# A fused attention and MLP kernel: PSUM banks from one pool, and an order chosen anew every four tiles

## The chip, the core and the metric

The kernel runs on one core of one Trainium2 chip. The core has TensorE (PE, matrix products into the accumulator memory PSUM), VectorE (DVE), ScalarE (ACT), GpSimd (POOL) and SyncE (SP, which issues the transfers). The engines run side by side, each taking its own instructions in the order in which the program wrote them, and they meet through semaphores. The metric is the device time of one execution in microseconds (us).

## The reference

One input `x` of 2048 rows by 512 goes through two branches that a gate mixes row by row:

```
x = A_x
g = sigmoid((x * gate_w).sum(-1))
a = attention(x, wqkv) @ wo          # 32 heads of 16, softmax over 2048 keys
h = gelu(layernorm(x) @ w1)          # then its quarters moved by 1, -1, 2, -2 rows
x1 = x + shifted(h) @ w2
b = x1 + gelu(layernorm(x1) @ w3) @ w4     # w3 is 512 x 1792
out = g * a + (1 - g) * b
```

Most of the work is the attention: 32 heads, each with 2048 x 2048 scores of which the exponential is taken and which are then multiplied by the values.

## The kernel before

The scores are cut into 2048 tiles of 128 keys by 512 queries, in 32 rounds of 64 tiles. A round is one chunk of 512 queries (`c`), one group of eight heads (`G`) and one parity (`p`), so four heads at a time: these lie in four row strips of PE. A score tile is one matmul over 32 rows (`qk_op`, L926 to L932), and two to four of them, in different strips, run at once. The products with the values and all projections use four column strips: four matmuls at a time, each into 32 partitions of one PSUM bank. Going from one kind to the other costs PE a pause, so the program gathers both kinds in groups.

A tile's exponential is made in one of two ways. `act_tiles` and `issue_act` (L940, L997) give two tiles to ScalarE, which turns 128x1024 scores at once into probabilities (L1009, tile `PA`); each tile then needs one matmul that adds its product with the values into the round's accumulator `acc` (L1104). `dve_tile` and `issue_dve` (L974, L1019) give one tile to VectorE, whose first pass (L1035) writes a linear function of the scores as 16-bit integers that, read as bf16, approximate a power of two. Two such tiles make a pair of 128x1024 in a buffer `PD`. `close_pair` (L1048) makes three more copies of the pair with a constant added (L1071 on VectorE, L1073 on POOL), and all four go into the accumulator with weights held in `V0` and `V2`: four matmuls per tile. Who makes the copies depends on two constants. Normally VectorE makes two and POOL makes the third out of the second. For a share `GP2` of the pairs (`both`), VectorE makes one and POOL makes two, straight from the first pass. Near the end of a round, and for a share 1 - `GP3`, VectorE makes all three (`alone`). At most three pairs are in work (`token`).

PSUM has eight banks. Before, they are fixed tiles: two tiles of two banks for ScalarE units (`psA`), three single banks (`ring`) for VectorE tiles and all projections, and `acc`. At the end of a round (`finish_round`, L1112) VectorE copies `acc` out (L1120); the next round's products may start when that copy is done (`acc_ready`). Transfers then spread the row sums, and POOL divides (L1137) and SP stores the heads into `oD`.

Around the attention lie the other products, each a generator of matmul groups (`gen`, L608) with the bank it needs, a place from which it may begin (`at`) and one by which it is due: transposes of `x`, projections to `q`, `k`, `v`, the gate, the MLP products `w1`, `w2`, `w3` and `w4` with the output projection. VectorE takes their results out of PSUM (`evac`, L625). ScalarE does GELU five times in large instructions.

The order of all this is decided when the program is built. The class `Sim` keeps a model of the five engines with a duration for each job (`hold`) and a latency, and steps through time: each engine takes the ready job of the best priority whose buffers are free, and `pe_pick` (L1268) decides what PE does next. First come scores for ScalarE when a unit's banks are free, together with tiles for VectorE while a ring bank is free and fewer than `DVE_WAIT` first passes wait; then, for as long as ScalarE is busy, projections and products with the values. Instructions are written out in the order of their modelled start. POOL's jobs and VectorE's copies within SBUF are marked `port`: the model never lets two of them overlap, and each POOL instruction waits for the last such VectorE instruction written before it (`in_port_order`, L158).

Some 25 constants (`BASE`) steer these choices: priorities, how many first passes may wait, how far tiles of the next round may go ahead, how full a group of products must be. A table `STAGES` replaces some of them for each 32 tiles.

Of the kernel before, what the change touches and what calls it, by code (L numbers as in the profile page):

```python
# [47 lines left out]

class Call:
# [6 lines left out]
class Job:  # L56
    __slots__ = ("eng", "hold", "lat", "deps", "prio", "fn", "acq", "frees", "at", "done", "start", "seq", "ready", "name", "port")

    def __init__(self, eng, hold, lat, deps, fn, prio=5, acq=(), frees=(), at=0, name="", port=False):
# [6 lines left out]
        self.name = name  # L66


class Op:
    __slots__ = ("mode", "tile", "fn", "done", "start", "ns", "frees", "name")  # L70

    def __init__(self, mode, tl, fn, ns=216.0, frees=(), name=""):
        self.mode, self.tile, self.fn, self.ns, self.frees = mode, tl, fn, ns, list(frees)
        self.done = self.start = None
        self.name = name


class Gen:


    def __init__(self, units, deps, at, name, acq="ring", due=None):
# [25 lines left out]
class Sim:  # L107
# [4 lines left out]
    def __init__(self, slots):  # L112
        self.free = {k: list(v) for k, v in slots.items()}
        self.jobs = {e: [] for e in ("ACT", "DVE", "POOL", "SP")}
        self.t_free = {e: 0.0 for e in ("ACT", "DVE", "POOL", "SP", "PE")}
# [12 lines left out]
        self.pelog = []  # L128

# [4 lines left out]
    def add(self, job):  # L134
        self.n += 1
        job.seq = self.n
        self.jobs[job.eng].append(job)
        self.pending += 1
        return job

    def take(self, b):
        b.slot = self.free[b.cls].pop(0)

    def release(self, bufs):
        for b in bufs:
# [4 lines left out]
            if b.users == 0:  # L150
                self.free[b.cls].append(b.slot)

# [16 lines left out]
    def finish_job(self, job):  # L169
        job.done = self.t  # L170
        self.release(job.frees)

    def try_engine(self, e):
        if self.t_free[e] > self.t:
            return False
        best = None
        for j in self.jobs[e]:
            if j.at > self.tiles:
                continue
            if j.ready is None:  # L180
                if any(d.done is None for d in j.deps):
                    continue
                j.ready = self.t
            if any(not self.free[b.cls] for b in j.acq) or j.port and self.lock > self.t:
                continue
# [10 lines left out]
        self.emit(self.t, self.in_port_order(e, j.fn) if j.port else j.fn)  # L196
# [10 lines left out]
    def pe_run(self, ops):  # L207
        cur = self.t
        for o in ops:
# [14 lines left out]
            self.emit(s, o.fn)  # L224
# [11 lines left out]
    def finish_op(self, o):  # L236
        o.done = self.t
        self.release(o.frees)

    def run(self, pe_pick, done):  # L240
        self.push(0.0, None)
        while self.events:
# [8 lines left out]
            while again:  # L251
                again = False
                for e in ("ACT", "DVE", "POOL", "SP"):
# [9 lines left out]
def kernel(  # L263
# [60 lines left out]
        SL=(45, 60),  # L324
# [10 lines left out]
        ROT=2, DUE_SH=-14, AT_SH=0, HOLE=7, MAXG=1,  # L335
    )
    SEG = 32
    STAGES = {
        0: {'DVE_WAIT': 1, 'DUE_SH': 32, 'P1_PRIO': 0.312, 'MAXU': 7},
        1: {'DVE_WAIT': 1, 'DUE_SH': 32, 'P1_PRIO': 0.312, 'MAXU': 7, 'URG_L': 18, 'AT_SH': 83, 'S_PRIO': 0.214},  # L340
        2: {'DVE_WAIT': 1, 'DUE_SH': 32, 'P1_PRIO': 0.312, 'MAXU': 7, 'URG_L': 18, 'AT_SH': 83, 'S_PRIO': 0.178, 'SL': (200, 200)},
# [1152 lines left out]
```

## Time and profile before

| | |
|---|---|
| three timed runs | 777.33, 780.11, 781.81 us |
| their median | 780.11 us |
| span of the profiled execution | 775.9 us |
| the profiled execution's own time | not on the page; the median run lies 4.2 us above its span |
| PE, DVE, ACT, POOL busy | 756.8, 725.7, 739.2, 364.9 us |
| granted TensorE clock | 1.000 |
| exponentials on ScalarE, first passes on VectorE | 742 (two tiles each, one of them half), 565 |
| shifted copies on VectorE, on POOL | 548, 301 |
| transfers | 34.60 MB, 45 GB/s |

The profile names a group of instructions by its line, its engine and the tiles it writes and reads (`PA<-psA`: writes PA, reads psA), with its count, its busy time and the mean of one, and then the idle time of the engine before it with the instruction that ended it. Durations run from an instruction's start until its result is written, so back-to-back instructions of one engine overlap, and the time that one holds its engine is the distance of two starts. Matmuls of different strips run at once, so PE's busy time says that something ran, not that the array was full. The chain is followed back from the last instruction, at each step to what released it.

### The profile page before, as it was taken

Reading aid. Unit: us, or ns where it says so; the run is one execution under the profiler, and the core shown is the slowest. Engines: PE = TensorE matmul, PEld = TensorE weight load, DVE = VectorE, ACT = ScalarE, POOL = GpSimd, SP = SyncE. Lnnn points to the kernel's source line nnn. Section 1 sums busy time; section 2 is a strip of 40 time slices with the busy share of each in tenths; the row PEclk is TensorE's granted clock in tenths of the full one; section 3 lists DMA queues with packets and bytes.
Section 4 is the critical chain, followed back from the end, with each engine's and each line's share of the span. In section 5 each row is a group of like instructions: output and inputs, shape, how many; then the busy total and the mean of one; then the engine's idle time right before and its main releaser. Section 6 shows DMA issues by size and latency. Waiting matters only on the chain.

```text
span 775.9 us, 23834 instructions
## 1 busy us (share of the span) xinstructions
PE 756.8 (98%) x9672; PEld 227.6 (29%) x9672; DVE 725.7 (94%) x1544; ACT 739.2 (95%) x767; POOL 364.9 (47%) x363
## 2 busy tenths in 40 slices
PE   9999999999999999999999999999999999999997
PEld 5433222222322222223222222422223222223222
DVE  6999999999999999999998999999999999998976
ACT  6799999999999999999998999998999999999995
POOL 2232443555457655344343464333584744436352
PEclk9999999999999999999999999999999999999999
DMA  9403321023000030041520002001100010000001
GB/s 191 142 30 78 71 79 41 19 45 116 20 6 20 19 71 20 20 126 29 124 47 24 23 20 47 27 24 26 40 20 19 16 34 14 26 19 20 17 17 35
DMA packets 67093, 34.60 MB, mean 45 GB/s; under 512 B 46748, under 2 KB 62380, under 8 KB 66984
## 3 DMA queue, kind: packets, MB, share of 16 engines
q1 hardware_dynamic: 66040, 32.56, 17.0%
q8 instruction: 75, 1.23, 0.7%
q10 hardware_dynamic: 944, 0.52, 0.2%
q14 instruction: 34, 0.28, 0.1%
HBM read 17.40 MB, written 6.81 MB: 31 GB/s over the span
## 4 chain that ended last, share of the span: by engine, by line
PE 61%; DVE 17%; ACT 14%; DMA 3%; issue 3%; POOL 1%; DVEq 0%; SPq 0%; POOLq 0%; ACTq 0%
PE acc L1104 21%; PE psA L929 20%; PE ring L615 18%; ACT PA L1009 10%; DVE PD L1035 6%; DVE PD L1071 5%; DMA xn_dram<-xn 1%; POOL PD L1073 1%; DVE st L762 1%; ACT hT L822 1%; DMA pk<-den 1%; ACT hB L853 1%; ACT hT L853 1%; PE ring L929 1%; DVE xn L782 1%
## 5 line engine op out<-in xcount | busy, mean ns | idle before, releaser
L1009 ACT ACTIVATE PA<-psA 128x1024 bf16<-128x1024 f32 x742 | 689.3, 1062 | 23.4 <-PE acc L1104 10.2
L1073 POOL TENSOR_SCALAR PD<-PD 128x1024 uint16<-128x1024 uint16 x301 | 311.8, 1045 | 373.5 <-DVE PD L1071 217.5
L1035 DVE TENSOR_SCALAR PD<-ring 128x512 uint16<-128x512 f32 x565 | 373.4, 683 | 20.0 <-PE ring L929 18.5
L1104 PE MATMUL acc<-PD,V 128*17 128x512 bf16 x2260 | 311.2, 381 | 2.3 <-POOL PD L1073 0.9
L929 PE MATMUL psA<-q,kT 32*128 32x512 bf16 x1483 | 286.8, 384 | 4.4 <-ACT PA L1009 3.8
L1104 PE MATMUL acc<-PA,V 128*17 128x512 bf16 x1483 | 271.0, 381 | 1.8 <-DVE accsb L1120 1.7
L1071 DVE TENSOR_SCALAR PD<-PD 128x1024 uint16<-128x1024 uint16 x548 | 222.2, 446 | 4.9 <-PE acc L1104 2.5
L929 PE MATMUL ring<-q,kT 32*128 32x512 bf16 x565 | 197.8, 384 | 0.5 <-DVE PD L1035 0.3
L929 PEld LDWEIGHTS <-kT 32*128 32x128 bf16 x2048 | 77.1, 91 | 306.6 <-issue 305.2
L1104 PEld LDWEIGHTS <-V 128*17 128x17 bf16 x3743 | 74.8, 88 | 131.7 <-issue 114.8
L615 PE MATMUL ring<-xnT,w 128*32 128x512 bf16 x1152 | 101.6, 383 | 0.8 <-DMA xnT<-xn_dram 0.8
L615 PE MATMUL ring<-w,hT 128*32 128x512 bf16 x704 | 66.8, 383 | 0.4 <-DVE w L874 0.3
L615 PEld LDWEIGHTS <-w 128*32 128x32 bf16 x1920 | 45.4, 95 | 47.8 <-issue 35.9
L1137 POOL TENSOR_TENSOR oT<-accsb,bcs 128x512 bf16<-128x512 f32 x31 | 39.5, 1273 | 17.8 <-DVE PD L1071 16.2
L615 PE MATMUL ring<-w,hB 128*32 128x512 bf16 x448 | 46.5, 383 | 0.0
L615 PE MATMUL ring<-w,w 128*32 128x256 bf16 (+1 forms) x768 | 38.4, 311 | 1.7 <-DVE PD L1035 1.3
L615 PE MATMUL ring<-wo,oD 128*32 128x512 bf16 x224 | 37.0, 383 | 1.7 <-DMA oD<-oT 1.7
L1120 DVE COPY accsb<-acc 128x512 f32<-128x512 f32 x31 | 21.2, 685 | 1.7 <-PE acc L1104 1.7
L615 PEld LDWEIGHTS <-hT 128*32 128x32 bf16 x704 | 16.4, 95 | 19.5 <-issue 15.7
L762 DVE BATCH_NORM_STATS2 st<-x_sb 128x6 f32<-128x512 bf16 x32 | 21.9, 687 | 0.1
L615 PE MATMUL ring<-w,wq 128*32 128x512 bf16 x256 | 20.7, 382 | 0.2 <-ACT w L646 0.2
L852 DVE CAST hT<-ring 128x512 bf16<-128x512 f32 x28 | 19.0, 681 | 1.2 <-PE ring L615 0.9
(93 smaller groups left out, 279.9 us busy)
## 6 DMA issues: line engine op xcount, KB each, us to landing
bcs<-rr SPq DMA_DIRECT2D x124, 64.0 KB
xn_dram<-xn SPq DMA_DIRECT2D x32, 128.0 KB
w<-in_B_w_dram SPq DMA_DIRECT2D x5, 512.0 KB
oD<-oT SPq DMA_DIRECT2D x124, 16.0 KB
w<-in_B_w_dram SPq DMA_DIRECT2D x4, 448.0 KB
out_dram<-ot SPq DMA_DIRECT2D x14, 128.0 KB
x_sb<-in_A_x_dram SPq DMA_DIRECT2D x3, 512.0 KB
w<-in_A_wqkv_dram SPq DMA_DIRECT2D x2, 256.0 KB
```

Source lines behind the costliest of these rows:

```text
L615: units.append([Op("col", j, lambda j=j, lf=lf, rf=rf, n0=n0, n1=n1, st=st, sp=sp: nc.tensor.matmul(get()[32 * j:32 * j + 32, n0:n1], lhsT ...
L762: a = dve(600, deps, lambda: nc.vector.bn_stats(out=sb.slot[:], in_=x_sb[:, t, :]), prio=6, at=at, acq=[sb])
L852: pre.append(evac(g, PSUM_NS, lambda ps, m=m: nc.vector.tensor_copy(out=h2()[:, m, :], in_=ps[:])))
L853: ge = act(93 + 427 * FT + 2600, pre, lambda: nc.scalar.activation(out=h2(), in_=h2(), func=ACT.Gelu_apprx_tanh), prio=0)
L929: o = Op("row", i, lambda: nc.tensor.matmul(dst(), lhsT=kT[G][32 * i:32 * i + 32, kt * P:(kt + 1) * P], rhs=qbuf[G, c].slot[32 * i:32 * i ...
L1009: job = act(hold, ops, lambda: nc.scalar.activation(out=pb.slot[:, 0:n], in_=buf.slot[:, 0:n], func=ACT.Exp, scale=0.25), acq=[pb], frees= ...
L1035: nc.vector.tensor_scalar(out=pr["buf"].slot[:, h * 512:(h + 1) * 512], in0=buf.slot[:], scalar1=BITS_MUL, scalar2=BITS_ADD, op0=ALU.mult, ...
L1071: return nc.vector.tensor_scalar(out=d[k][:, 0:w], in0=d[0][:, 0:w], scalar1=float(SHIFT * k), scalar2=None, op0=ALU.add)
L1073: return nc.gpsimd.tensor_scalar(out=d[k][:, 0:w], in0=d[0 if both else 2][:, 0:w], scalar1=1.0, scalar2=float(SHIFT * (k if both else 1)) ...
L1104: o = Op("col", i, lambda: nc.tensor.matmul(acc[32 * i:32 * i + DH + 1, :], lhsT=lhs(), rhs=rhs(), start=st, stop=True, tile_position=(0, ...
L1120: e = dve(PSUM_NS, round_ops[r], lambda: nc.vector.tensor_copy(out=ab.slot[:], in_=acc[:]), acq=[ab], prio=0)
L1137: n = gp(1250, d3, lambda: nc.gpsimd.tensor_tensor(out=ob.slot[:], in0=ab.slot[:], in1=bb.slot[:], op=ALU.mult), acq=[ob], frees=[ab, bb], ...
```

## The change

PSUM becomes one pool of eight banks, numbered 0 to 7. A ScalarE unit takes two neighbouring free banks (`Run`), a VectorE tile, a projection or an accumulator takes any one. The limits are constants: four banks in ScalarE units (`CAP2`), three for tiles and projections (`LIMD`), one accumulator at a time (`ACC2` is 0), taken when a round's first product is issued and given back when VectorE has copied it out; the next round's accumulator may take another free bank meanwhile. Since the pool's banks are not tiles of the framework any more, `guard` adds the wait of a bank's first writer for the readers of its last holder. Units of three banks and first passes over two tiles (`CAP3`, `JOIN`) can be written with the new functions, but their constants are 0 throughout.

Probabilities of ScalarE lie in sixteen slots of 512 columns in place of eight of 1024. An exponential takes any two free slots, and each is free again when its own product has been issued and done.

The first product of a round in each column strip writes 32 partitions in place of 17, so that no row of the bank is left from an earlier holder; where the next head's columns do not exist, a matmul with zero weights clears them first.

The table of 65 rows (32 tiles each) gives way to one of 497 steps for 512 stretches of four tiles, in which a constant stays until a step changes it. The mean over all tiles of `GP2` goes from 0.16 to 0.77, of `MAXU` (groups that PE takes at a time) from 8.0 to 4.4; others move less. The functions that make the copies, the planner's durations and the amount of other work stay as they are.

```diff
+class Run:
+    def __init__(self, cls, n):
+        self.cls, self.n = cls, n
+        self.bufs = [Buf(cls, 1) for _ in range(n)]
...
+    def fits(self, b):
+        if isinstance(b, Run):
+            return b.pick(self.free[b.cls]) is not None
+        return bool(self.free[b.cls])
...
-    SEG = 32
-    STAGES = {
-        0: {'DVE_WAIT': 1, 'DUE_SH': 32, 'P1_PRIO': 0.312, 'MAXU': 7},
...
+    SEG = 4
+    STEPS = {
+        0: dict(P1_PRIO=0.279, GP2=1, DVE_STOP=8, URG=8, DVE_ALONE=-158, IDLE_NS=864, DVE_WAIT=1, AHEAD=7, AHEAD2=16,
+            PRESS=15, MAXU=5, MAXG=2),
...
-    WIDTHS, RING = (2, 2), 3
+    NBANK = 8
...
-    acc = ps.tile([P, 512], F32, name="acc")
+    accs = {}
...
-        **{f"psA{w}{n}": slots(f"psA{n}", 1, [P, 512 * w], F32, ps) for n, w in enumerate(WIDTHS)},
-        "ring": sim_ring,
-        "PA": slots("PA", NPA, [P, 512 * max(WIDTHS)]),
+        "bank": list(range(NBANK)),
+        "PA": list(range(2 * NPA)),
...
+    def guard(b, inst):
+
+        if b not in held_by.setdefault(b.slot, []):
+            for old in held_by[b.slot]:
+                for x in sim.readers.get(old, []):
+                    tc.add_manual_dep(inst.ins, x.ins.name, mybir.DependencyInfo(
+                        mybir.DependencyClass.Sync, mybir.DependencyReason.DATA), reason="bank")
+            held_by[b.slot] = [b]
...
-        job = act(hold, ops, lambda: nc.scalar.activation(out=pb.slot[:, 0:n], in_=buf.slot[:, 0:n], func=ACT.Exp,
-                                                          scale=0.25), acq=[pb], frees=[buf], prio=3)
+        job = act(hold, ops, lambda: nc.scalar.activation(out=pa_all[:, pb.cut(), :], in_=unit()[:, rb.cut(), :],
+                                                          func=ACT.Exp, scale=0.25), acq=[pb],
+                  frees=rb.bufs + [Call(lambda: act_done(w))], prio=3)
...
+    def acc_ok(r):
+        if r in accs:
+            return True
+        if r > acc_round[0] + K.ACC2 or not sim.free["bank"]:
+            return False
+        return r == acc_round[0] or others() + acc_banks[0] < K.LIMA
...
+            n = 32 if st and not edge else DH + 1
+            if edge:
+                sim.guard(accs[r], nc.tensor.matmul(one(accs[r])[32 * i:32 * i + 32, :], lhsT=zero[:, 0:32], rhs=rhs(),
+                                                    start=True, stop=True, tile_position=(0, 32 * i), skip_group_check=True))
...
-        e = dve(PSUM_NS, round_ops[r], lambda: nc.vector.tensor_copy(out=ab.slot[:], in_=acc[:]), acq=[ab], prio=0)
-        acc_ready[0] = e
-        acc_round[0] = r + 1
+        e = dve(PSUM_NS, round_ops[r], lambda: nc.vector.tensor_copy(out=ab.slot[:], in_=one(accs[r])), acq=[ab], prio=0,
+                frees=[accs[r], Call(acc_done)])
```

More of the change, by code (lines that the diff above doesn't have):

```diff
@@ L180, in try_engine @@
             if j.ready is None:
[L181 to L182 removed]
                 j.ready = self.t
[L184 removed]
+            if j.port and self.lock > self.t or j.acq and any(not self.fits(b) for b in j.acq):
                 continue
@@ L1225, in gen_new @@
     def gen_new():
-        if not sim.free["ring"]:
+        if not room():
             return None
```

1044 lines of the change are left out of this document (886 added, 158 removed).

## The prediction

> **What bounds the kernel now.** I read the page first: busy shares, the engine split of the chain, the costliest groups.
>
> ```profile
> span 775.9 us, 23834 instructions
> PE 756.8 (98%) x9672; PEld 227.6 (29%) x9672; DVE 725.7 (94%) x1544; ACT 739.2 (95%) x767; POOL 364.9 (47%) x363
> PE 61%; DVE 17%; ACT 14%; DMA 3%; issue 3%; POOL 1%; DVEq 0%; SPq 0%; POOLq 0%; ACTq 0%
> L1009 ACT ACTIVATE PA<-psA 128x1024 bf16<-128x1024 f32 x742 | 689.3, 1062 | 23.4 <-PE acc L1104 10.2
> L1073 POOL TENSOR_SCALAR PD<-PD 128x1024 uint16<-128x1024 uint16 x301 | 311.8, 1045 | 373.5 <-DVE PD L1071 217.5
> L1035 DVE TENSOR_SCALAR PD<-ring 128x512 uint16<-128x512 f32 x565 | 373.4, 683 | 20.0 <-PE ring L929 18.5
> L1071 DVE TENSOR_SCALAR PD<-PD 128x1024 uint16<-128x1024 uint16 x548 | 222.2, 446 | 4.9 <-PE acc L1104 2.5
> ```
>
> Three engines are nearly full and one, POOL, is half empty. The 2048 score tiles are divided 1483 to ScalarE (742 exponentials) and 565 to VectorE (283 pairs, 849 shifted copies: 548 by VectorE, 301 by POOL).
>
> Then the time line, for what an instruction holds its engine: durations of back-to-back ones overlap, so starts are compared. Last, busy time in four stretches (columns: stretch, its length, PE, PEld, DVE, ACT, POOL, granted clock, DMA share, GB/s).
>
> ```profile
> 250.85 94.74 ACT L1009 ACTIVATE PA<-psA 128x1024 bf16<-128x1024 f32 x103 [0.18 <-PE acc L1104]
> 398.29 1.28 DVE L1035 TENSOR_SCALAR PD<-ring 128x512 uint16<-128x512 f32 x2
> 269.79 1.08 DVE L1071 TENSOR_SCALAR PD<-PD 128x1024 uint16<-128x1024 uint16 x3
> ```
> ```profile
> 20.00:180.00 160.00, 156.77 (x2079) 49.41 (x2075) 154.97 (x351) 152.09 (x165) 64.16 (x64) 1.00 0.27 72
> 180.00:360.00 180.00, 176.63 (x2141) 50.97 (x2138) 178.44 (x390) 179.68 (x183) 97.60 (x96) 1.00 0.15 37
> 360.00:540.00 180.00, 176.04 (x2282) 51.43 (x2277) 167.81 (x354) 171.82 (x180) 77.38 (x73) 1.00 0.16 39
> 540.00:760.00 220.00, 217.28 (x2749) 62.01 (x2742) 202.21 (x404) 214.95 (x220) 118.04 (x113) 1.00 0.09 23
> ```
>
> An exponential holds ACT for (94.74 - 1.06)/102 = 0.918 us, a first pass holds DVE for 1.28 - 0.68 = 0.60, a shifted copy for (1.08 - 0.42)/2 = 0.33. So ACT needs 742 x 0.918 = 681 us, and 50 for GELU, table loads and copies (739.2 - 689.3): 731 of 775.9. Of the other 45 us, 23.4 stand before units by the page, and the rest is start and end. From 180 to 360 us ACT has no gap at all: there only fewer ACT tiles can save time. Early (20 to 180) ACT lacks 8 us, DVE is 97% full, POOL 40%; later ACT and DVE both have holes.
>
> PE's 98% overstates: in the chain a row group of two score matmuls takes 0.32 us and eight column matmuls 0.54, twelve 0.76. With some 6,900 column matmuls (acc 3743; L615 1152, 704, 448, 256, 224 and half of the 768 narrow ones) to 742 units (9.3 each, 0.61 us) it needs 0.93 us a unit, 690 us. By the Trainium skill (Perfetto Trace Analysis, Identifying the Most-Contended Engine) matmul busy time is no measure of PE's headroom, and the weight loads' share is: 29% here would leave PE out of it, and the sum would then be that of the full relief below, 747; the starts, which leave PE 11%, decide for me.
>
> **The change, part by part.**
>
> 1. *Which copies POOL makes.* The code that makes the three copies is the same, but its constant GP2, the share of pairs of which POOL makes two and DVE one, averages 0.16 over the tiles before and 0.77 after (0.88, 0.86, 0.97 in the first three eighths, against 0.00, 0.08, 0.41). At 283 pairs that is 0.61 x 283 = 173 copies moved: DVE loses 173 x 0.33 = 57 us, POOL gains 173 x 1.045 = 181 us (365 to 546). DVE can spend the 57 us on more tiles, at 0.60 + 0.33 x (2 - 0.77)/2 = 0.80 us each: at most 71 tiles, which take 71/2 x 0.918 = 33 us from ACT. On PE such a tile costs three more accumulating matmuls (3 x 0.054, a twelve less an eight being 0.22 for four) and saves half a unit's two switches and row group: about nothing. Does it convert? Two neighbouring stretches of before hold 161 score matmuls each, 227.0 to 281.3 us with the share at 0.65, and 281.3 to 335.7 us with 0.00:
>
> ```profile
> L1035 DVE TENSOR_SCALAR PD<-ring 128x512 uint16<-128x512 f32 x39 | 26.1, 683 | 0.0
> L1071 DVE TENSOR_SCALAR PD<-PD 128x1024 uint16<-128x1024 uint16 x28 | 10.8, 436 | 0.0
> L831 DVE TENSOR_TENSOR x_sb<-x_sb,ring 128x512 bf16<-128x512 bf16 x13 | 8.7, 680 | 0.1
> L762 DVE BATCH_NORM_STATS2 st<-x_sb 128x6 f32<-128x512 bf16 x12 | 8.2, 690 | 0.1
> ```
> ```profile
> L1035 DVE TENSOR_SCALAR PD<-ring 128x512 uint16<-128x512 f32 x45 | 29.9, 686 | 0.4 <-PE ring L929 0.3
> L1071 DVE TENSOR_SCALAR PD<-PD 128x1024 uint16<-128x1024 uint16 x45 | 17.4, 434 | 0.0
> L852 DVE CAST hB<-ring 128x512 bf16<-128x512 f32 x11 | 7.5, 686 | 0.0
> ```
>
> The first kept the rate of the second with some 8 us more of other DVE work, but with 6 tiles fewer, not more. So the relief is real and converts in part. Ends: 0 and -33; I take half, **-16**, because port and PE (below) leave no room for all.
>
> 2. *The port.* DVE's SBUF copies and POOL's work exclude one another, and line 158 makes POOL wait for the last such DVE instruction:
>
> ```profile
> 622.78 1.27 POOL L1137 TENSOR_TENSOR oT<-accsb,bcs 128x512 bf16<-128x512 f32 x1 [0.54 <-DMA bcs<-rr]
> 622.89 2.46 DVE L1071 TENSOR_SCALAR PD<-PD 128x1024 uint16<-128x1024 uint16 x4
> ```
>
> Four copies take 2.46 us beside that, not 0.42 + 3 x 0.33 = 1.41: 1.05 lost. Mean against median of all 548 (446, 420 ns) makes 14 us blocked in all. With 474 POOL copies for 301 and 375 DVE ones for 548 the meetings stay about as many (1.57 x 0.68 = 1.08), but each holds up DVE's queue, first passes behind it, and so PE's banks. Ends 0 and +14; **+3**.
>
> 3. *Order chosen per 4 tiles.* No instruction is added; what can go is ACT's wait, 10.2 + 5.9 + 5.1 = 21 us behind PE. Ends: -21, and +21 if the finer order fits the chip worse than the planner's durations say. Those durations are as good as here (0.833 x 1024 + 67 = 920 ns in the code, 918 measured; 598 and 600), so it should fit: a third, **-7**.
>
> 4. *Banks.* Limits stay: 4 banks in ScalarE units, 3 others, 1 accumulator. A unit now needs two neighbouring free banks of eight: PE's wait for a unit is 3.8 us now (psA behind ACT); it might go or double: **+2**. A bank's first writer waits for the readers of its last holder, as it did for its fixed tile. The accumulator of the next round may open in another bank while DVE still copies the last: PE's wait for that copy is 2.0 us in all, ends 0 and -2 (the copy's 0.69 us x 31 is covered by score and projection matmuls, else it would cost 21): **-1**.
>
> 5. *Single release of probabilities.* Sixteen half slots for eight whole ones; ACT writes two that need not adjoin. No row shows ACT waiting on a slot apart from the 10.2 us behind the accumulating matmuls, counted in 3: 0 (ends -3, +3). The first matmul of a round in each quarter writes 32 columns, not 17 (a weight load is 88 ns for 17, 95 for 32: 120 x 7 ns, hidden), eight rounds add one matmul (8 x 0.054), and a memset of 0.5 us in the start-up goes: 0. No DMA is moved: SP's queue sees the same issues, later or earlier with their rounds.
>
> Sum: -16 + 3 - 7 + 2 - 1 = -19: a span of 757. The timed runs stand at 777.33 to 781.81, median 780.11, 4.2 above the span of the profiled execution; so **761 us**, within 751 to 770 when the half in part 1 comes out between four fifths and a fifth.
>
> **The rivals.**
>
> *The port becomes the bound (slower).* Busy now: POOL 365, DVE copies 548 x 0.33 = 181, other SBUF-only DVE work about 40 (xn 12.7, q 11.1, pk 6.1, x_sb 6.0, V 3.6): 586 of 776. After, at the same pairs: 546 + 124 + 40 = 710, and between a DVE copy's end (398.38) and the POOL copy that it lets go (398.53) lie 0.15 us, 283 times: 752. Nothing here runs over 95% full (ACT, of the engines whose times are not modelled), so 752/0.95 = 792, and 796 as measured. It decides once a pair's turn of the port outlasts its share of the span, 776/283 = 2.74 us: two POOL copies, one DVE copy and the gap make 2 x 1.045 + 0.33 + 0.15 = 2.57, before normalising and the round's multiply, 1.27. PE takes its work in order, so a late copy would stop scores too. Against it: in 227 to 281 us POOL copies fill 30.7 of 54.3 us and ACT never waits over 0.2. The Trainium skill (SBUF — State Buffer, Who interferes with whom) calls the shared pair an exclusive lock under which the later one fully blocks; by that rule the 792 is what a full port gives, and the trace agrees with the lock (1.05 us lost above).
>
> *Full conversion.* All 71 tiles move: 775.9 - 33 + 4 = 747 as measured. For: POOL stands at 40% in the first 180 us, where DVE is full. Against: the port, and PE, whose 690 are 93% of that span of 743.
>
> *It does not do what it says.* Tiles divide as before, the waits move elsewhere: 780, 776 to 784. For: the stretch at 0.65 above, with 39 DVE tiles and the same rate.
>
> **How the numbers follow.** Forecast 0.52, port 0.18, full conversion 0.18, no effect 0.12. 0.5%, about 4 us, is what a measurement of this kernel can tell from none. Faster: 0.52 + 0.18 + 0.03 = 0.73; same 0.05; slower 0.18 + 0.04 = 0.22. The range goes from 747 (half of the full conversions lie below, 0.09) to 790 (over half of the port's cases above, 0.11).
>
> **What would show it.** Right: POOL near 500 busy or more, with 420 or more copies at the POOL line; under 730 exponentials; under 450 DVE copies; ACT at 96% or more and its wait behind PE under 18 us; the span shorter mostly before 360 us, where GP2 rises most. Wrong: 742 or more exponentials; DVE copies' mean well over 446 ns (the port); accumulating matmuls of PE that wait for POOL's copies (0.9 us now) by 10 us or more; psA waits behind ACT far over 3.8 (banks lying apart).

## The result, and the profile after

| | before | after |
|---|---|---|
| median of the timed runs | 780.16 us (774.45 to 783.9) | 776.79 us (774.1 to 779.82) |
| ratio, 95% interval | | 0.9961, 0.9943 to 0.9979 |
| span of the profiled execution | 775.9 us | 774.0 us |

The change makes the kernel 3.4 us faster, where 19 were forecast. First the page of the changed kernel: busy shares, the engine split of the chain, and the four groups shown of before (each with count, busy time, mean of one, idle time before it and what ended most of it).

```profile
span 774.0 us, 23775 instructions
PE 757.5 (98%) x9623; PEld 224.1 (29%) x9623; DVE 718.8 (93%) x1403; ACT 736.6 (95%) x762; POOL 528.5 (68%) x524
PE 70%; DVE 18%; issue 4%; DMA 3%; POOL 2%; ACT 2%; SPq 1%; DVEq 0%; POOLq 0%; ACTq 0%
L1743 ACT ACTIVATE pa_all<-banks 128x1024 bf16<-128x1024 f32 x737 | 686.6, 1059 | 21.8 <-PE banks L1648 13.5
L1813 POOL TENSOR_SCALAR PD<-PD 128x1024 uint16<-128x1024 uint16 x462 | 475.3, 1052 | 209.8 <-DVE PD L1811 84.5
L1773 DVE TENSOR_SCALAR PD<-banks 128x512 uint16<-128x512 f32 x574 | 374.9, 676 | 23.0 <-PE banks L1648 20.2
L1811 DVE TENSOR_SCALAR PD<-PD 128x1024 uint16<-128x1024 uint16 x399 | 193.5, 526 | 2.2
```

POOL took over the copies as forecast (462 for 301), and DVE makes 149 fewer. But DVE's copies got dearer, 526 ns in the mean for 446, so the 149 are worth only 29 us of its busy time (222.2 to 193.5). And DVE does only nine tiles more (574 for 565), so ACT is spared five exponentials: 5 x 0.918 = 4.6 us. Its idle time before them is still 21.8 us.

Busy time by stretches (stretch, length, PE, PEld, DVE, ACT, POOL, granted clock, DMA share, GB/s):

```profile
20.00:180.00 160.00, 157.81 (x2120) 47.85 (x2114) 153.33 (x326) 155.44 (x169) 111.98 (x111) 1.00 0.29 73
180.00:360.00 180.00, 175.13 (x2093) 49.09 (x2086) 174.88 (x353) 172.84 (x172) 133.36 (x131) 0.98 0.18 47
360.00:540.00 180.00, 178.53 (x2223) 49.72 (x2221) 162.99 (x313) 177.01 (x186) 117.27 (x113) 1.00 0.13 30
540.00:760.00 220.00, 217.88 (x2806) 64.14 (x2802) 207.83 (x377) 211.92 (x216) 157.74 (x152) 1.00 0.09 22
```

From 180 to 360 us ACT, which had no gap there before, now lacks 7 us, and the granted clock is 0.98. DVE, with fewer copies to make, still fills 153 and 175 us of the first two stretches.

A second reading needs the program's plan. The planner gives every score matmul a start; its order is kept on the chip, so the n-th one in the trace can be set beside the n-th one planned. The plan ends at 773.1 us before and at 752.5 after: a gain of 20.6. The trace stands ahead of (-) or behind (+) it, in us, by:

| score tile | 0 | 448 | 896 | 960 | 1408 | 2048 |
|---|---|---|---|---|---|---|
| before | -0.8 | -1.7 | -4.2 | -4.4 | -3.2 | -5.9 |
| after | +0.3 | +2.5 | +4.6 | +9.7 | +11.4 | +13.0 |

After the last score tile both lose the same 8.5 us. So the plan's gain is given back in two ways: a jump of 5.1 us between tiles 896 and 960, and a slow drift. Before goes from -0.8 to -5.9, -5.1 in all; after, without the jump, from +0.3 to +7.9. At the end that is 7.9 + 5.9 = 13.8 us of difference, 1.1 of them from the start. 20.6 - 5.1 - 13.8 leaves 1.7; the spans differ by 1.9.

**The jump.** The time line of the changed kernel around 340 us (start, duration, engine, line; in brackets the idle time before and its end; SPq lines are issues of transfers):

```profile
330.20 0.33 SPq L1898 DMA_DIRECT2D bcs<-rr  x1
330.57 2.38 SPq L1281 DMA_DIRECT2D w<-in_B_w_dram  x4
333.01 1.76 SPq L1898 DMA_DIRECT2D bcs<-rr  x3
...
340.69 1.28 POOL L1901 TENSOR_TENSOR oT<-accsb,bcs 128x512 bf16<-128x512 f32 x1 [3.28 <-DMA w<-in_A_x_dram]
341.03 3.90 DVE L1811 TENSOR_SCALAR PD<-PD 128x1024 uint16<-128x1024 uint16 x4
...
343.53 0.39 PE L1865 MATMUL banks<-PD,V 128*17 128x512 bf16 x3 [1.62 <-POOL PD L1813]
...
345.95 1.02 ACT L1743 ACTIVATE pa_all<-banks 128x1024 bf16<-128x1024 f32 x1 [3.19 <-PE banks L1648]
```

The four loads of the w4 weights (1.8 MB) went into the queue between the first and the other three transfers of a round's `bcs`. POOL's multiply, which needs `bcs`, waits 3.28 us. (The view names the transfer issued next behind them, `w<-in_A_x_dram`, as the end of this wait: it landed at 340.63, the last `bcs` at 340.43. With all four `bcs` ahead of the weights, in a run below, no transfer is waited for.) POOL takes its work in order, so the copies behind it are late; DVE's four copies take 3.90 us in place of 1.41; PE waits for POOL's copies, ACT for PE.

That wait is not the whole jump. Behind it PE was granted only half of its clock, from 344.2 to 351.0 us in this trace (columns as above):

```profile
345.00:350.00 5.00, 5.00 (x37) 0.80 (x35) 2.51 (x4) 3.53 (x4) 4.71 (x5) 0.50 0.35 78
```

A score matmul takes 603 ns there, 384 before. The last score tile ahead of the wait stands 4.5 us behind the plan, the first after it 7.7, the first after the clock's return 10.0: some 3 us of the jump came with the wait and some 2 with the clock. The timed runs differ along the same line: of the twenty, the three with a mean granted clock of 0.999 have spans of 772.3 to 773.0 us, the five with 0.990 to 0.992 have 775.2 to 778.0.

**The drift.** An early piece, POOL and DVE only:

```profile
121.82 3.07 POOL L1813 TENSOR_SCALAR PD<-PD 128x1024 uint16<-128x1024 uint16 x3 [1.21 <-PE banks L1648]
123.96 1.54 DVE L1811 TENSOR_SCALAR PD<-PD 128x1024 uint16<-128x1024 uint16 x2
125.66 2.06 POOL L1813 TENSOR_SCALAR PD<-PD 128x1024 uint16<-128x1024 uint16 x2 [0.76 <-PE banks L1648]
127.22 1.44 DVE L1811 TENSOR_SCALAR PD<-PD 128x1024 uint16<-128x1024 uint16 x3
128.81 2.06 POOL L1813 TENSOR_SCALAR PD<-PD 128x1024 uint16<-128x1024 uint16 x2 [1.10 <-DVE PD L1811]
```

The port goes to and fro without a pause. DVE's pair of copies at 123.96 was issued while POOL still worked and took 1.54 us in place of 0.75, the three at 127.22 took 1.44 in place of 1.08. POOL begins 0.16 us after DVE's last copy has ended (125.50 to 125.66, 128.66 to 128.81). The plan frees the port 338 ns after a copy's start; on the chip it is 420 + 156 = 576, so POOL is 0.24 us late at each such turn. DVE copies of over 480 ns that end right behind POOL number 44 before and 100 after; all copies together lie 14 and 42 us above 420 ns each.

### The profile page after: what moved, and what is told of

It reads as the page before. It is cut to its first block, busy times and chain, and to the rows that moved or that the text cites. A ratio compares the mean times of both kernels' runs of the same rounds, so it can differ in the third digit from the quotient of the medians.

```text
span 774.0 us, 23775 instructions
## 1 busy us (share of the span) xinstructions
PE 757.5 (98%) x9623; PEld 224.1 (29%) x9623; DVE 718.8 (93%) x1403; ACT 736.6 (95%) x762; POOL 528.5 (68%) x524
## 4 chain that ended last, share of the span: by engine, by line
PE 70%; DVE 18%; issue 4%; DMA 3%; POOL 2%; ACT 2%; SPq 1%; DVEq 0%; POOLq 0%; ACTq 0%
PE banks L1865 23%; PE banks L1648 23%; PE banks L1330 21%; DVE PD L1773 8%; DVE PD L1811 6%; POOL PD L1813 2%; ACT pa_all L1743 2%; DMA pk<-den 1%; SPq L1905 1%; DMA w<-in_A_x_dram 1%; DVE pk L1892 0%; PE banks L1309 0%; PE banks L2195 0%; DVE accsb L1885 0%; DVE q L1403 0%
## 5 line engine op out<-in xcount | busy, mean ns | idle before, releaser
L1743 ACT ACTIVATE pa_all<-banks 128x1024 bf16<-128x1024 f32 x737 | 686.6, 1059 | 21.8 <-PE banks L1648 13.5
L1813 POOL TENSOR_SCALAR PD<-PD 128x1024 uint16<-128x1024 uint16 x462 | 475.3, 1052 | 209.8 <-DVE PD L1811 84.5
L1773 DVE TENSOR_SCALAR PD<-banks 128x512 uint16<-128x512 f32 x574 | 374.9, 676 | 23.0 <-PE banks L1648 20.2
L1865 PE MATMUL banks<-PD,V 128*17 128x512 bf16 (+1 forms) x2296 | 302.7, 383 | 6.5 <-POOL PD L1813 4.5
L1648 PE MATMUL banks<-q,kT 32*128 32x512 bf16 x2048 | 300.7, 386 | 2.5 <-DVE PD L1773 1.5
L1865 PE MATMUL banks<-pa_all,V 128*17 128x512 bf16 (+1 forms) x1474 | 262.6, 383 | 0.0
L1811 DVE TENSOR_SCALAR PD<-PD 128x1024 uint16<-128x1024 uint16 x399 | 193.5, 526 | 2.2
L1865 PEld LDWEIGHTS <-V 128*17 128x17 bf16 (+1 forms) x3770 | 74.6, 88 | 129.3 <-issue 110.4
L1330 PE MATMUL banks<-xnT,w 128*32 128x512 bf16 x1152 | 93.5, 385 | 1.3 <-DVE PD L1773 0.9
L1330 PE MATMUL banks<-w,hT 128*32 128x512 bf16 x704 | 62.1, 383 | 0.3 <-DVE PD L1773 0.2
L1901 POOL TENSOR_TENSOR oT<-accsb,bcs 128x512 bf16<-128x512 f32 x31 | 39.5, 1274 | 22.7 <-DVE PD L1811 13.9
L1330 PE MATMUL banks<-w,hB 128*32 128x512 bf16 x448 | 41.5, 383 | 0.0
L1330 PEld LDWEIGHTS <-hT 128*32 128x32 bf16 x704 | 16.4, 95 | 20.8 <-issue 12.2
```

The costliest lines, as they stand in the source:

```text
L1330: units.append([Op("col", j, lambda j=j, lf=lf, rf=rf, n0=n0, n1=n1, st=st, sp=sp: nc.tensor.matmul(get()[32 * j:32 * j + 32, n0:n1], lhsT ...
L1648: o = Op("row", i, lambda: nc.tensor.matmul(dst(), lhsT=kT[G][32 * i:32 * i + 32, kt * P:(kt + 1) * P], rhs=qbuf[G, c].slot[32 * i:32 * i ...
L1743: job = act(hold, ops, lambda: nc.scalar.activation(out=pa_all[:, pb.cut(), :], in_=unit()[:, rb.cut(), :], func=ACT.Exp, scale=0.25), acq ...
L1773: return nc.vector.tensor_scalar(out=pr["buf"].slot[:].rearrange("p (b c) -> p b c", c=512)[:, h0:h0 + w, :], in0=unit()[:, rb.cut(), :], ...
L1811: return nc.vector.tensor_scalar(out=d[k][:, 0:w], in0=d[0][:, 0:w], scalar1=float(SHIFT * k), scalar2=None, op0=ALU.add)
L1813: return nc.gpsimd.tensor_scalar(out=d[k][:, 0:w], in0=d[0 if both else 2][:, 0:w], scalar1=1.0, scalar2=float(SHIFT * (k if both else 1)) ...
```

## The experiments

Two theories were open for the lost 19 us. *Port*: DVE's freed time goes into waiting for the port, which POOL now holds longer and which changes hands dearer than planned. *Banks*: the pool of eight banks or the finer order costs PE time that the planner does not see. Where copies of POOL are cut short, the columns that they don't write are the part of the result that is left out.

### Short copies on POOL, in both kernels

```diff
-                return nc.gpsimd.tensor_scalar(out=d[k][:, 0:w], in0=d[0 if both else 2][:, 0:w], scalar1=1.0,
+                return nc.gpsimd.tensor_scalar(out=d[k][:, 0:64], in0=d[0 if both else 2][:, 0:64], scalar1=1.0,
```

Changed kernel:

> The changed kernel with its order untouched, but POOL's shifted copies cover 64 columns in place of 1024 (most of their values are left out; the copy buffers are cleared once at the start). Port theory: the order planned with many POOL copies falls behind on the chip because a turn of the port shared by VectorE's copies and POOL takes longer there than the planner allows; without long POOL copies the time falls by 12 to 18 us, to 758 to 765. Bank theory (waits of a bank's first writer, neighbours not free): nothing is taken from it, 770 to 777. VectorE's copies, 526 ns now, go to about 430 either way.

Kernel before:

> The same cut in the kernel before, whose 301 POOL copies leave the port free a quarter of the time. Port theory: little to win, 0 to 5 us, 775 to 780. If short POOL copies are worth 12 us or more here as well, the cost is not special to the new order and the port theory, as an account of the difference, falls.

Measured: 759.95 us for the changed kernel (0.9771 of before, 0.9741 to 0.98), 780.11 for the one before (1.0027, 1.0004 to 1.0049). Both clear the copies' buffers at the start, which moves their first score tile back by 2.8 us (changed kernel) and 4.7 us (before). The groups of the changed kernel with short copies:

```profile
L1745 ACT ACTIVATE pa_all<-banks 128x1024 bf16<-128x1024 f32 x737 | 679.5, 1125 | 11.2 <-PE banks L1650 5.4
L1815 POOL TENSOR_SCALAR PD<-PD 128x64 uint16<-128x64 uint16 x462 | 104.3, 244 | 528.0 <-DVE PD L1813 265.9
L1813 DVE TENSOR_SCALAR PD<-PD 128x1024 uint16<-128x1024 uint16 x399 | 151.9, 425 | 2.9 <-DVE PD L1775 0.5
```

With the same order and the same 737 exponentials, ACT's idle time halves (21.8 to 11.2), DVE's copies fall back to 425 ns, and the trace goes from 3.1 us behind its plan to 2.7 ahead, a drift of -5.8 like before's -5.1, without a jump. What the change loses hangs on POOL's copies. The kernel before loses little by them: with the late start it is 2 us slower, and its drift goes from -5.1 to -6.6, so short copies are worth 1.5 us to it by the drift. The jump is gone too: a POOL that is not loaded absorbs the late `bcs`.

### One part alone: pooled banks with the old table, and the old kernel with more copies on POOL

The first keeps the pool of banks and single release, and takes back the table of 65 rows:

```diff
-    SEG = 4
-    STEPS = {
+    SEG = 32
+    STAGES = {
```

> The new kernel's banks, single slots and accumulators with the old table of constants (32 tiles a row, the share GP2 at 0.16). The planner inside the program ends its own clock at 789.5 us for it, against 773.1 for the kernel before and 752.5 for the changed one; the traced spans of those two are 775.9 and 774.0, so 2.8 and 21.5 us over. Port theory: few POOL copies, so the chip keeps to the plan, 2 to 5 us over in span, 795 to 799 as timed. Bank theory: the pool is what the chip pays for, 15 us or more over, 808 or more.

The second is the kernel before with one constant:

```diff
-        GP2=0.0,
+        GP2=0.6,
```

(and 0.6 in the rows that set it).

> The kernel before, fixed banks, with GP2 at 0.6 in every row: 446 to 470 POOL copies as in the changed kernel. Its planner ends at 782.5 us. Port theory: the chip falls behind as with the changed kernel, 10 to 18 us over the plan in span, 796 to 804 as timed. Bank theory: fixed banks keep to the plan, 2 to 5 us over, 788 to 791.

Measured: 791.73 us (1.0176, 1.0144 to 1.0209) and 796.13 (1.0234, 1.02 to 1.0269). Pooled banks with the old table have a worse plan, 789.5 us, and the chip is even 2.1 us faster than it (span 787.4, score tiles 8.2 ahead at the end), where both theories had it slower: the banks cost nothing on the chip that the planner doesn't know, and the theory of the banks falls. What the pool is worth in the plan is another matter: with the old table it makes the plan 16.4 us longer (773.1 to 789.5), and no run has the fine table without the pool. The kernel before with 405 copies on POOL was planned at 782.5 and came out at a span of 794.1, over its plan as the theory of the port said. But by tiles its excess is not a drift: it keeps the slope of the kernel before, and loses 10.4 us at one place, between tiles 896 and 960 again, where w4 loads stand in the queue too, and where PE waited 3.3, 1.0 and 1.2 us and was granted half of its clock for 17.1. So this run does not show a price of the port, and its place called for the next.

### The w4 loads later

The four loads are written 8 us later, behind the round's `bcs` transfers:

```diff
+        if name[0] == "4":
+            late.append(fn)
...
+    sim.order[:] = [(t + 8000.0 if fn in late else t, n, fn) for t, n, fn in sim.order]
     sim.order.sort(key=lambda x: (x[0], x[1]))
```

> The changed kernel with one shift: the four loads of the 1.8 MB of w4 weights are written 8 us later in the order, behind the last three of the round's four bcs transfers; everything else, the plan with its 752.5 us too, stays. In the changed kernel those three transfers stand behind the weights in the queue, POOL's multiply of 340.69 us waits 3.28 us for one of them, and copies, accumulating matmuls, scores and exponentials follow late: the trace falls some 5 us further behind the plan between score tiles 896 and 960. Theory of the queue (that transfer is the cause of this step): the step goes, the multiply in that stretch waits under 1 us, the time falls by about 5 us to 771 to 773. Theory of the port alone (the chip falls behind because the port changes hands dearer than planned, and the weights only lie beside it): the multiply runs earlier, but the step stays or comes back within 50 us, 775 to 778.

Measured: 772.03 us (0.9926, 0.9903 to 0.9949), span 767.4. The same place in this kernel's time line:

```profile
329.05 1.72 SPq L1902 DMA_DIRECT2D bcs<-rr  x4
...
332.15 11.28 ACT L1747 ACTIVATE pa_all<-banks 128x1024 bf16<-128x1024 f32 x12 [0.27 <-PE banks L1652]
332.44 2.17 SPq L1283 DMA_DIRECT2D w<-in_B_w_dram  x3
...
336.92 1.27 POOL L1905 TENSOR_TENSOR oT<-accsb,bcs 128x512 bf16<-128x512 f32 x1 [0.69 <-DVE PD L1815]
```

The four `bcs` transfers are together, the multiply waits 0.69 us for the port and not for a transfer, ACT has no gap, and the lag between tiles 896 and 960 stays at 3.4 us. The granted clock stays at 1.00 through this stretch too. The jump was the queue, with the halved clock that came behind its wait. The drift is still there (from 0.0 to +6.2 at the end).

The same shift in the kernel before with GP2 at 0.6:

> The kernel before with the share GP2 at 0.6 in all rows (796.13 us), with the same shift of the four w4 loads by 8 us; the plan of 782.5 us stays. That kernel followed its plan as the kernel before does, up to one step of 10.4 us between score tiles 896 and 960, where four transposes for the projections stood behind the 1.8 MB of weights in the queue. Theory of the queue: the step goes, 785 to 788, some 10 us less, and the trace ends its score tiles 4 to 8 us ahead of the plan as in the kernel before (5.9 ahead). Theory that more copies on POOL as such make the chip fall behind the plan (405 for 301): the step stays or shows elsewhere, 792 to 797.

Measured: 794.57 us (1.023, 1.0209 to 1.0251). Here the theory of the queue missed: the step shrinks from 10.4 to 9.2 us only. The time line of that kernel shows another transfer in the same place:

```profile
335.90 10.36 SPq L796 DMA_TRANSPOSE xnT<-xn_dram  x4
...
343.00 0.38 PE L619 MATMUL ring<-xnT,w 128*32 128x512 bf16 x1 [1.78 <-DMA xnT<-xn_dram]
343.97 1.94 ACT L1013 ACTIVATE PA<-psA 128x1024 bf16<-128x1024 f32 x2 [1.92 <-PE psA L933]
```

PE waits for transposed rows, and ACT for PE, with or without the weights ahead of them; and behind these waits its clock is granted at half again, for 6.8 us from 345.0 and 3.4 from 358.7. What makes these transposes late in that order stays open. That more copies as such make the chip fall behind (the other expectation, 792 to 797) fits the number, but not the shape: a step is no drift.

### POOL without the wait for the port

```diff
-            elif inst is not None and self.last_port is not None:
+            elif False:
```

> The changed kernel without the dependency that makes a POOL instruction wait for the last DVE instruction that uses the shared port (line 273); the order of both engines stays, and POOL still waits for data. Measured in the changed kernel, a POOL copy starts 156 ns after the traced end of the DVE copy that it waits for, and the plan has this turn about 0.24 us cheaper. Theory that the price of a turn is the wait by semaphore: POOL copies then start with the end of the DVE copy or earlier, some 150 turns that stand on DVE's path save up to 0.05 to 0.15 us each, and the time falls by 4 to 12 us, to 765 to 773. Theory that the price is the exclusion itself (whoever comes later is held until the other has done): without the dependency POOL takes the port ahead of DVE copies that the plan has first, each DVE copy caught so takes 1 us more; mean of a DVE copy over 560 ns (526 in the changed kernel), time 777 or more, up to 790.

With the later loads as well:

> Both edits at once: the w4 loads 8 us later and no dependency of POOL on DVE's last instruction at the port. If the two causes are separate, the differences of the two single runs against the changed kernel add up within 2 us; if the step at 340 us is only the place where a delay of the port comes to light, the later loads gain nothing more once the dependency is gone. Queue theory with a cheap turn: 762 to 768; queue theory with the exclusion as the price: the time of the run without the dependency less 5.

Measured: 840.84 us (1.0796, 1.0768 to 1.0824) and 837.66 (1.0766, 1.0725 to 1.0807); the two edits add up within 2 us. The loss is far beyond the 777 to 790 that even the second theory allowed. The groups without the wait:

```profile
L1743 ACT ACTIVATE pa_all<-banks 128x1024 bf16<-128x1024 f32 x737 | 695.0, 1050 | 75.0 <-PE banks L1648 66.7
L1813 POOL TENSOR_SCALAR PD<-PD 128x1024 uint16<-128x1024 uint16 x462 | 500.4, 1103 | 251.4 <-DVE PD L1773 76.6
L1811 DVE TENSOR_SCALAR PD<-PD 128x1024 uint16<-128x1024 uint16 x399 | 242.0, 647 | 2.2
```

Both engines now catch each other at the port (DVE's copies 647 ns, POOL's 1103), and a DVE copy that comes second stops the first passes behind it: ACT idles 75 us before its exponentials. PE stops often, and its clock is granted at half for 30.7 us of this trace, against 6.8 in the changed kernel; that is a part of the 64 us. So the wait is not what the turn costs; it keeps a far larger loss away. The Trainium skill (SBUF — State Buffer, Who interferes with whom) says that issue order decides who blocks, and that the loser is held for the whole instruction; the trace agrees for DVE, whose held copies end 279 ns after POOL's end, so that one caught early takes over 1 us.

### How short must a copy be?

All kernels from here on have the later w4 loads. POOL's copies with 512 of 1024 columns, with 768, and whole but made by two instructions of 512:

```diff
+                for a in range(0, w, 512):
+                    one_of = nc.gpsimd.tensor_scalar(out=d[k][:, a:a + 512], in0=d[0 if both else 2][:, a:a + 512], scalar1=1.0,
...
```

> The changed kernel with the w4 loads 8 us later (772.03 us), in which POOL's copies write 512 of 1024 columns (the other halves keep zeros, so this part of the result is left out); the order stays. A copy of POOL then takes some 0.6 us in place of 1.05 and 0.24 for 64 columns (759.95 us). Theory that the price goes with the time POOL holds the port: half way, 764 to 768, DVE copies' mean 460 to 485 ns (526 and 425 at the ends). Theory of a price per turn of the port, whatever its length (there are as many turns as with long copies): but little gained, 769 to 772. Theory that only a POOL that is late with its own work costs: nearly all gained, 759 to 762.

> As the run with half copies (758.08 us, of which a copy took 618 ns), but with 768 of 1024 columns (the last quarter keeps zeros, so this part is left out): some 0.83 us a copy, 0.22 less than in full. Theory of slack: a turn of the port costs about 0.24 us more than planned, a copy that is 0.22 shorter just about pays for it, and most of the 14 us goes: 758 to 762, DVE copies' mean under 450 ns. Theory that the price goes with the time POOL holds the port: half way between 758 and 772, 764 to 767, mean 460 to 485 ns.

> The changed kernel with the w4 loads 8 us later (772.03 us), in which POOL makes each of its copies by two instructions of 512 columns in place of one of 1024: the whole result, the same order, but POOL holds the port for at most 0.6 us at a stretch and needs 462 x 0.2 = 92 us more in all (a half copy takes 618 ns, a whole one 1047). Theory that DVE's copies are held up by the length of the one POOL instruction that they meet: their mean falls from 516 to under 480 ns, time 765 to 771. Theory that POOL itself is late, because the plan leaves no slack behind its copies: POOL is busy 615 us, its lateness grows, mean of a DVE copy 550 ns or more, time 785 to 810.

| columns | one instruction | time | ratio, interval | mean of DVE's copies |
|---|---|---|---|---|
| 1024 | 1047 ns | 772.03 us | 0.9926, 0.9903 to 0.9949 | 516 ns |
| 768 | 832 | 759.21 | 0.9761, 0.9738 to 0.9784 | 433 |
| 512 | 618 | 758.08 | 0.9757, 0.974 to 0.9774 | 425 |
| 2 x 512 | 640 twice | 800.43 | 1.0289, 1.0265 to 1.0313 | 579 |

The two short ones clear the copies' buffers at the start, and their first score tiles come 2.8 us (768) and 1.6 us (512) late. From there to the last tile their drift is -6.4 and -6.3 us, that of 64 columns is -5.8, and whole copies have +6.2. So the price is not proportional to the time that POOL holds the port: 0.21 us less per copy takes all of it away, and a further 0.21 changes nothing more.

Nor is it the length of the one instruction that DVE meets: cut in two, POOL holds the port for 0.64 us at a stretch, and everything is worse, since it needs 565.1 us for 473.8. In the plan 393 of POOL's 462 copies begin the moment that another instruction of POOL or a copy of DVE ends, 101 of them behind a copy of DVE (129 and 44 of the 301 before). So there is little slack; each turn is up to 0.24 us dearer than planned, POOL falls behind, and DVE and PE wait for it. A copy that is 0.21 shorter pays for the turn. The 57 turns more, at 0.24, make 13.7 us; this is an estimate, since not every late turn need reach the end. That POOL lacks slack is what these lengths show; that it is the turn which uses it up is argued, since no kernel was planned with the dearer turn.

The groups of the kernel with 768 columns, then of the one with copies in two pieces:

```profile
L1749 ACT ACTIVATE pa_all<-banks 128x1024 bf16<-128x1024 f32 x737 | 679.3, 1126 | 10.8 <-PE banks L1654 5.2
L1817 DVE TENSOR_SCALAR PD<-PD 128x1024 uint16<-128x1024 uint16 x399 | 155.3, 433 | 2.2
```

```profile
L1752 ACT ACTIVATE pa_all<-banks 128x1024 bf16<-128x1024 f32 x737 | 693.7, 1045 | 39.5 <-PE banks L1657 30.1
L1820 DVE TENSOR_SCALAR PD<-PD 128x1024 uint16<-128x1024 uint16 x399 | 214.9, 579 | 2.2
```

### Copies given back to VectorE

If POOL only lacks slack, some of its copies can go back to DVE at full length, in places where DVE stood idle in the plan while POOL worked. Plan and order stay:

```diff
+    for j, pr, k in copies:
+        a, b, idle = j.start, j.start + j.hold, 0.0
...
+        if idle + max(0.0, b - a) >= 338:
+            swap.add((id(pr), k))
...
+                if (id(pr), k) in swap:
+                    sim.swapped = True
+                    return nc.vector.tensor_scalar(out=d[k][:, 0:w], in0=d[0 if both else 2][:, 0:w],
```

With thresholds of 338, 250 and 200 ns these are 68, 129 and 204 of the 462:

> The changed kernel with the w4 loads 8 us later (772.03 us), in which 68 of POOL's 462 copies are given back to VectorE: those during which the plan has VectorE idle for at least the 338 ns that its own copy would take; the plan and the order are those of the changed kernel, and the whole result is made. Theory of slack (POOL is late because each of its turns at the port costs some 0.24 us more than planned): POOL loses 71 us of work at places where VectorE only waited for the port, catches up there, and most of the 14 us of delay goes: 760 to 766. Theory that VectorE's time is what counts and its idle time in the plan is not there on the chip: 68 x 0.33 = 22 us more work on VectorE, 775 to 785.

> The same with 129 copies given back, those with at least 250 ns of planned idle time of VectorE (POOL then makes 333 copies, nearly as few as the 301 of the kernel before). Theory of slack: as with 68, or 1 to 2 us faster or slower, 758 to 767, since VectorE has room for 43 us where it waited for the port. Theory that VectorE's time is what counts: twice the price of the 68, 780 to 795.

> The same with 204 copies given back, those with at least 200 ns of planned idle time of VectorE. A copy holds VectorE for 330 ns, so the last 75 of them find 200 to 250 ns of room and cost VectorE 75 x 0.1 = 8 us beyond what stood idle, in places where it is the bound up to all of that. Theory that POOL's slack alone counts: 762 to 765, as with 129. Theory that the point is passed at which VectorE's time takes over: 767 to 773.

Measured: 766.16 us (0.9843, 0.9815 to 0.987), 763.98 (0.9818, 0.9791 to 0.9845) and 768.34 (0.9858, 0.9828 to 0.9888). The groups with 129 given back (L1824 are these), then two with 204:

```profile
L1752 ACT ACTIVATE pa_all<-banks 128x1024 bf16<-128x1024 f32 x737 | 682.3, 1092 | 15.4 <-PE banks L1657 8.8
L1826 POOL TENSOR_SCALAR PD<-PD 128x1024 uint16<-128x1024 uint16 x333 | 342.4, 1045 | 292.2 <-DVE PD L1820 119.3
L1820 DVE TENSOR_SCALAR PD<-PD 128x1024 uint16<-128x1024 uint16 x399 | 162.4, 448 | 1.2
L1824 DVE TENSOR_SCALAR PD<-PD 128x1024 uint16<-128x1024 uint16 x129 | 55.6, 433 | 0.0
```

```profile
L1752 ACT ACTIVATE pa_all<-banks 128x1024 bf16<-128x1024 f32 x737 | 685.1, 1068 | 17.5 <-PE banks L1657 10.0
L1824 DVE TENSOR_SCALAR PD<-PD 128x1024 uint16<-128x1024 uint16 x204 | 85.1, 418 | 0.0
```

The first two agree with the theory of slack, 68 copies at the very end of its range (760 to 766). 129 copies cost DVE 55.6 us of busy time and give it back 27.6 (190.0 to 162.4) in copies that are no longer held; POOL has 131 us less to do; the trace ends its score tiles 0.9 us behind the plan in place of 6.2. At 204 the gain shrinks (span 767.3 for 762.0; the intervals of the ratios still touch), and DVE is 95% busy: POOL would have slack enough by then, and DVE's time count, which is argued. With 129 the kernel makes its whole result in 763.98 us: faster than both kernels, with POOL making 333 copies, 32 more than before the change, not 161.

## Why the prediction was wrong

The sign was right and the time lies in the range, but 3.4 us came for 19, and that both held is luck: three terms came out 5 to 11 us worse than forecast, and one 9 us better kept the sign. By the plan and the traces the tiles gave -4.6 for -16, the rest of the plan's gain -16 for -7 (20.6 less 4.6), the drift +13.8 for +3 and the jump +5.1 for nothing. By its own steps:

1. *Which copies POOL makes, -16: this step failed.* The move itself is as worked out (149 copies for 173, POOL busy 528.5 for 546). But the 57 us of DVE were to become up to 71 tiles, half of them taken; nine came, 4.6 us. Already in the plan, DVE's idle time rises from 81 to 106 us, and in 52 of the 106 a copy is ready while POOL holds the port (22 of the 81 before): of the 49 us that the 149 copies would have held it, DVE waits for 30. The kernel before with GP2 at 0.6 shows the step by itself: 104 copies moved, the tiles stayed at 565 and the exponentials at 742, and it was 16 us slower, 9.4 of them already in its plan (782.5 for 773.1). The stretch at a share of 0.65 with six tiles fewer, which the step showed, was the better guide than the half that I took.
2. *The port, +3: mis-sized, and with the wrong reason.* Ends were 0 and +14; the runs give 12.8 (768 columns) to 13.9 us (512) against whole copies, near the upper end, as the kernel before loses 1.5 itself. "The meetings stay about as many" is what failed: held copies went from 44 to 100. I multiplied counts as if POOL's and DVE's turns met by chance; here each pair of DVE's copies waits for POOL by design, and POOL comes late to each turn. What decided, as far as the copies of other lengths tell, was not how full the port is but that the plan had no slack for a turn that is 0.24 us too cheap in it.
3. *Order per four tiles, -7: right in direction, hidden.* ACT's idle time before its exponentials fell by 1.6 us only (23.4 to 21.8); with the loads later it is 17.0, with 768 columns 10.8, a gain of 12.6. The plan is 20.6 us shorter with hardly more DVE tiles, so most of the change's worth was in the order (with the pool of banks, which no run takes apart from it), not in step 1. One part of it the traces show on PE, which step 3 did not look at: 733 groups of score matmuls for 743, and 1888 steps of four column matmuls for 1912, which at the prediction's 0.32 us a group and 0.22 a step is some 8 us less, an estimate. Whether PE would then stop it short of the 747 of a full relief stays open: the shortest span of all runs is 756.3 (512 columns), with 11.0 us of idle time left before the exponentials. That those durations "are as good as here" and that "it should fit" holds for ACT and DVE alone; the turn of the port and the queue of transfers are not in those durations.
4. *Banks, +2 and -1: no wait to see, worth open.* All waits of PE's score matmuls are 2.5 us after, and pooled banks with the old table stay within their plan. But that plan is 16.4 us longer than the one before, and the run 11.6 us slower (791.73); with the new table their share is not known.
5. *Single release, 0:* no row speaks against it.

What the sum lacked was the queue. No transfer was added, and I never asked which small transfer might come to stand behind which large one. "SP's queue sees the same issues, later or earlier with their rounds" was true and not harmless: 1.8 MB of weights came to lie between four small transfers, 5.1 us by the plan's table, some 2 of them PE's halved clock (2.7 by the ratios, 4.8 by the medians, 6.6 by the spans).

Of the rivals, "no effect, 780" came nearest, with tiles divided as before; but the gain did not fail to arise, it was lost again. The port as the bound (796) did not come; the kernel with copies in two pieces, with 91 us more work on POOL, came to 800. Of the signs, POOL's busy time and copies, DVE's copies under 450 and ACT's share came near or true. 737 exponentials for under 730, and some 19 us of ACT's waits behind PE (13.5 and 5.2 are the largest) for under 18, missed; nor did the gain lie before 360 us: score tile 896 came 2.9 us earlier than before the change, tile 960 4.2 us later. DVE's copies at 526 ns were the named sign of a wrong prediction by the port.

## What to carry to other kernels

A finer plan can use up the slack that covered the faults of its model: before trusting its gain, look for what the model leaves out (here a turn of a shared port, 0.24 us, and small transfers behind large loads), and set the trace beside the plan event by event, so that a drift and a jump can be told apart. Moving work to an idle engine is worth what the other engine can do with the time, not the time itself; where both share a lock, the best share can lie well short of the most that the idle one could take (here 333 copies did better than 462). Cutting an operation by a quarter, without regard for the result, tells cheaply whether a stage is bound by an engine's time or only lacks slack.

## What the runs showed of the hardware

- A POOL instruction that waits by semaphore for a DVE copy begins 156 to 157 ns after that copy's end in the traces before and after (the median; 84 at the least), and a DVE copy held by POOL ends 278 to 279 ns after POOL's end.
- Without that wait the kernel takes 64 us more, as both engines are then caught: 647 ns in the mean for a DVE copy of 420, 1103 for a POOL copy of 1045.
- A POOL copy of 64, 512, 768 and 1024 columns takes 244, 618, 832 and 1047 ns: some 0.84 ns a column, and 190 that do not depend on the columns. Two halves cost a fifth more than a whole (565.1 for 473.8 us).
- `bcs` transfers of 64 KB each, issued behind 1.8 MB of weights at 333.01 us and after, let their reader begin at 340.69; without the weights between them they are done before it asks.
- Behind PE's wait that ended at 343.53 us its clock was granted at half for 6.8 us, and a score matmul took 603 ns for 384: some 2 us more, on top of the 3 that came with the wait. In the run without this wait the granted clock stayed at 1.00 there.
